# Four small loads ahead of q's, in a linear-attention and feed-forward kernel on one Trainium2 core

## The chip, the cores and the metric

The kernel runs on one core of one Trainium2 chip. The metric is the device time of one execution in microseconds; lower is better. Engines are called as the profile calls them: PE is TensorE (matmuls; PEld is its weight load), DVE is VectorE, ACT is ScalarE, POOL is GpSimd, SP is SyncE, which here issues loads and stores.

## The reference

Inputs are q, k, v of shape (8, 8, 576, 64), w_in of (512, 2048) and w_out of (2048, 512), all float32. What is computed:

```
q_s = softmax(q) over the 64 columns          k_s = softmax(k) over the 576 rows
kv  = einsum('bhsd,bhse->bhde', k_s, v)
a   = einsum('bhsd,bhde->bhse', q_s, kv)
x   = a.transpose(0, 2, 1, 3).reshape(4608, 512)
h   = x @ w_in ;  g = h * sigmoid(h) ;  out = g @ w_out
```

## The kernel before

A batch of q, k or v is loaded in two halves of four heads each (`load`, lines 146 to 150): 128 partitions with two rows of 9 x 64 floats, 576 KB. For each half the exponentials are taken on ACT (`exp_q` L161, `exp_k` L166), q's row sums and their reciprocals on DVE (L205, L209), and q is scaled by them (L214); v is cast to bfloat16 with a column of constants beside it (`vcast`, L142 and L144). q is transposed on PE (L232) and copied out of PSUM (`trcopy`), the products k x v follow on PE (L246), then they are divided by k's sums (`kvcopy`, L257 and L259), multiplied by q (L280) and copied as x into XT (`xt_evac`).

The feed-forward part then works on x in nine chunks of 512 tokens, with the first batch's 576 columns as an exception (`wide_mm`, L305, 16 blocks of 128 columns of w_in). From the second chunk on, both matrix products are done in seven block products in place of eight (L423, L501), so DVE makes sums and differences of weights and inputs. Weights are held as float16: their loads cast from float32 and are issued by POOL (`load_w1` L562, `load_w2` L568).

The order of all work is written by hand: the head is plain code (lines 543 to 619), and behind it the string ORDER names one operation after the other. In the head, SP issues six loads of the first batch one behind the other: q's two halves, k's first, v's first, k's second, v's second. All six go through one hardware queue. ACT starts with the load of its table and an exponential of one element, `dummy`. POOL makes the identity matrix for the transposes and then copies one element of k's first half into `gate` (L577), which holds its queue until that half has landed; only then it issues the five loads of w_in, then q's loads of the second batch, w_out and so on. PE runs matmuls on a tile of zeros (`heat`, L559) in its idle stretches: 20 at the start, then 7, 3 and 2 between the steps of the first batch.

The tile h1 is one of three scratch tiles of 128 x 1024 floats in the pool `mp`. In the kernel before it is first written at L186, at 30.29 us.

Of the kernel before, what the change touches and what calls it, by code (L numbers as in the profile page):

```python
# [8 lines left out]
FP32 = mybir.dt.float32  # L9
# [61 lines left out]
def kernel(  # L71
# [9 lines left out]
    nc = tc.nc  # L81
# [9 lines left out]
    TCH = 512  # L91
# [15 lines left out]
    mp = ctx.enter_context(tc.tile_pool(name="mp", bufs=2))  # L107
# [38 lines left out]
    def load(b, name, src, cc, eng):  # L146
        t = ld.tile([128, 2, J * D], FP32, name=name)
        st[b][name, cc] = t
        x = src[b].rearrange("(g r) (p j) d -> g (r p) (j d)", r=2, j=J)
        eng.dma_start(out=t, in_=x.rearrange("g x y -> x g y")[:, 2 * cc:2 * cc + 2, :])  # L150
# [391 lines left out]

    nc.vector.memset(dummy, 0.0)
    nc.vector.memset(warm, 0.0)
    nc.scalar.activation(out=dummy, in_=dummy, func=ACT.Exp)
    make_identity(nc, ident_f)
    for name, src in (("qt", q), ("kt", k)):
        load(0, name, src, 0, nc.sync)
        if name == "qt":
            load(0, name, src, 1, nc.sync)  # L550
# [154 lines left out]
    for t in range(1, NCH):  # L705
# [6 lines left out]
        for g in range(2):  # L712
            n = f"{t}.{g}."
# [123 lines left out]
```

## Time and profile before

| | us |
|---|---|
| median of 3 runs (258.03 to 258.7) | 258.57 |
| the profiled execution | 258.52 |
| its span, first to last instruction | 256.5 |
| PE busy | 248.3 (97%) |
| DVE busy | 205.5 (80%) |
| ACT busy | 190.9 (74%) |
| POOL busy | 66.3 (26%) |
| moved by DMA | 45.89 MB, mean 179 GB/s |

PE's share is that of matmuls in flight, the ones on zeros among them. The granted TensorE clock is full in all 40 slices of the span. In the page's chain of work that ended last, PE has 50% of the span and "issue", time in which an engine waited for nothing that the profile shows, 32%. The DMA engines are busy, with short dips, from about 2 to 48 us. A share of DMA time above 1 means that packets overlap on an engine.

### The profile page before, as it was taken

The page shows a single profiled execution, that of the slowest core. Times are in us where ns is not written, and L with a number is a line of the kernel's source. Part 1 is how long each engine was busy: PE and PEld are TensorE (multiplying, and loading weights), DVE is VectorE, ACT ScalarE, POOL GpSimd, SP SyncE. Part 2 cuts the span into 40 slices and gives each one's busy share as a digit, 9 for nine tenths or more (in the row PEclk, how much of TensorE's full clock was granted, in tenths as well). Part 3 has the DMA queues.
Part 4 walks back from the last instruction along what each step waited for, and adds up shares of the span by engine and source line. Part 5 has one row for each costly group of instructions (what it writes and reads, how often), then busy time and mean ns, then how long its engine had stood idle before and what let it go on. Part 6 is the DMA issues. An engine that isn't in the chain of part 4 may idle for free.

```text
span 256.5 us, 6456 instructions
## 1 busy us (share of the span) xinstructions
PE 248.3 (97%) x2732; PEld 204.3 (80%) x2732; DVE 205.5 (80%) x276; ACT 190.9 (74%) x225; POOL 66.3 (26%) x64
## 2 busy tenths in 40 slices
PE   8799999999999999999999999999999999999992
PEld 3367746757888888888888888888888888888881
DVE  2858999987999989998998986996569837886750
ACT  4766876998999999999879979736597557565211
POOL 1653592630541440430082040006000000000023
PEclk9999999999999999999999999999999999999999
DMA  7999999979969928995956850030807000700454
GB/s 249 344 180 296 302 301 301 347 162 393 365 162 266 400 87 216 361 306 127 310 223 110 218 202 0 3 82 3 174 3 164 3 0 4 164 3 0 87 130 113
DMA packets 35900, 45.89 MB, mean 179 GB/s; under 512 B 16240, under 2 KB 20912, under 8 KB 35872
## 3 DMA queue, kind: packets, MB, share of 16 engines
q1 hardware_dynamic: 29328, 33.50, 44.8%
q0 software_dynamic: 6224, 11.73, 17.9%
q8 instruction: 21, 0.34, 0.5%
q10 hardware_dynamic: 320, 0.26, 0.5%
q14 instruction: 7, 0.06, 0.1%
HBM read 36.70 MB, written 9.44 MB: 180 GB/s over the span
## 4 chain that ended last, share of the span: by engine, by line
PE 50%; issue 32%; DVE 6%; DMA 5%; POOL 5%; ACT 0%; POOLq 0%; DVEq 0%; ACTq 0%
PE PS L423 21%; PE PS L501 19%; DMA qt<-in_q_dram 5%; PE PS L443 4%; PE PS L333 2%; POOL eq L214 2%; PE PS L246 2%; POOL W L562 1%; POOL out_dram L789 1%; PE PS L280 1%; DVE S L475 1%; DVE XS L381 1%; DVE GT L321 1%; DVE XT L144 1%; DVE zq L205 0%
## 5 line engine op out<-in xcount | busy, mean ns | idle before, releaser
L401 DVE TENSOR_TENSOR h<-PS,h 128x1024 f32<-128x1024 f32 (+1 forms) x45 | 54.1, 1204 | 8.9 <-PE PS L423 7.9
L501 PEld LDWEIGHTS <-GT 128*128 128x128 f16 x512 | 50.1, 98 | 5.9
L423 PEld LDWEIGHTS <-WS 128*128 128x128 f16 x480 | 46.7, 98 | 6.5 <-issue 0.6
L407 ACT ACTIVATE GT<-h 128x1024 f16<-128x1024 f32 (+1 forms) x45 | 46.8, 1049 | 1.0 <-DVE h L401 0.7
L501 PE MATMUL PS<-W,GT 128*128 128x256 f16 x384 | 47.3, 273 | 0.0
L423 PE MATMUL PS<-XS,WS 128*128 128x256 f16 (+1 forms) x360 | 45.0, 272 | 0.0
L142 ACT COPY h<-PS 128x1024 f32<-128x1024 f32 (+1 forms) x31 | 31.1, 1004 | 17.1 <-PE PS L423 16.0
L501 PEld LDWEIGHTS <-S 128*128 128x128 f16 x384 | 37.1, 98 | 4.6
L423 PEld LDWEIGHTS <-W 128*128 128x128 f16 x360 | 35.2, 98 | 4.4
L214 POOL TENSOR_TENSOR eq<-eq,rzq 128x1152 bf16<-128x1152 bf16 x13 | 27.4, 2117 | 37.8 <-DVE rzq L209 37.0
L501 PE MATMUL PS<-T,S 128*128 128x256 f16 x256 | 32.2, 273 | 0.0
L144 POOL CAST vaug<-vt 128x1152 bf16<-128x1152 f32 x12 | 15.5, 1306 | 60.4 <-DMA vt<-in_v_dram 59.6
L423 PE MATMUL PS<-XT,W 128*128 128x256 f16 (+1 forms) x240 | 29.7, 272 | 0.0
L144 DVE COPY h<-PS 128x1024 f32<-128x1024 f32 (+1 forms) x14 | 17.0, 1213 | 8.8 <-PE PS L423 3.9
L205 DVE TENSOR_REDUCE zq<-eq 128x18 f32<-128x1152 bf16 x14 | 18.8, 1341 | 4.1 <-ACT eq L161 3.9
L789 POOL DMA_DIRECT2D out_dram<-ow x7 | 3.8, 542 | 70.6 <-DVE ow L771 70.0
L161 ACT ACTIVATE eq<-qt 128x1152 bf16<-128x1152 f32 (+1 forms) x18 | 18.8, 1054 | 2.7 <-DMA qt<-in_q_dram 2.5
L166 ACT ACTIVATE ek<-kt 128x1152 bf16<-128x1152 f32 x16 | 18.6, 1162 | 1.8 <-DMA kt<-in_k_dram 1.7
L407 ACT ACTIVATE GT<-PS 128x1024 f16<-128x1024 f32 (+1 forms) x15 | 15.2, 1013 | 6.1 <-PE PS L423 6.1
L501 PE MATMUL PS<-T,GT 128*128 128x256 f16 x128 | 16.3, 273 | 0.0
L501 PE MATMUL PS<-W,S 128*128 128x256 f16 x128 | 16.1, 273 | 0.0
L305 PE MATMUL PS<-XT,W 128*128 128x288 f16 x128 | 15.9, 286 | 0.0
(85 smaller groups left out, 331.0 us busy)
## 6 DMA issues: line engine op xcount, KB each, us to landing
out_dram<-ow SPq DMA_DIRECT2D x64, 128.0 KB, 2.7
qt<-in_q_dram SPq DMA_DIRECT2D x12, 576.0 KB, 6.0
kt<-in_k_dram SPq DMA_DIRECT2D x12, 576.0 KB, 7.2
vt<-in_v_dram SPq DMA_DIRECT2D x12, 576.0 KB, 6.9
qt<-in_q_dram POOLq DMA_DIRECT2D x4, 576.0 KB, 10.1
kt<-in_k_dram POOLq DMA_DIRECT2D x4, 576.0 KB, 13.1
vt<-in_v_dram POOLq DMA_DIRECT2D x4, 576.0 KB, 11.8
W<-in_moe_w_in_dram POOLq DMA_DIRECT2D x3, 512.0 KB, 10.5
```

The costliest lines, as they stand in the source:

```text
L142: eng.copy(out=o, in_=i)
L144: eng.tensor_copy(o, i)
L161: nc.scalar.activation(out=half(st[b]["eq"], cc)[:, :, g0:g1], in_=jgd(b, "qt", cc)[:, :, g0:g1], func=ACT.Exp)
L166: nc.scalar.activation(out=half(ek, cc), in_=jgd(b, "kt", cc), func=ACT.Exp)
L205: nc.vector.reduce_sum(out=z, in_=e, axis=AX.X)
L214: eng.tensor_tensor(out=e, in0=e, in1=r[:, :, :, None].to_broadcast([128, J, 2, D]), op=ALU.mult)
L305: nc.tensor.matmul(out=PS[:, WIDE[fb] + n, 0:S // 2], lhsT=W1[:, c, fb * 128:(fb + 1) * 128], rhs=XTS[0][:, c, n * (S // 2):(n + 1) * (S / ...
L401: nc.vector.tensor_tensor(out=four(t, i), in0=group_bank(t, g), in1=four(t, i), op=ALU.add)
L407: nc.scalar.activation(out=group_out(t, f, n), in_=x, func=ACT.Silu, scale=1.0 / XS)
L423: nc.tensor.matmul(out=PS[:, bank + p // 2, (p % 2) * HT:(p % 2) * HT + width(t)], lhsT=a[:, c, p * 128:(p + 1) * 128], rhs=bb[:, c, 0:wid ...
L443: nc.tensor.matmul(out=PS[:, 2 + tb, :], lhsT=GTS[t % 2][:, fc, tb * 128:(tb + 1) * 128], rhs=W2[:, fc, :], start=(fc == 0), stop=(fc == N ...
L501: nc.tensor.matmul(out=PS[:, bank, m * HN:(m + 1) * HN], lhsT=a[:, fc, m * 128:(m + 1) * 128], rhs=bb[:, fc, :], start=(first and fc == 0) ...
```

## The change

Four loads are added at the head of the kernel. Each reads 16 floats (64 bytes) from 16 places: of k's first batch (the first row of each half head, 16 places 72 KB apart), of w_in (every 32nd row, 256 KB apart), of w_out (every 128th row, 256 KB apart) and of v's first batch (as k). They go into 16 partitions of the tile h1, 64 columns in all, and nothing reads them. ACT issues those of k and w_in, ahead of its table load; POOL issues those of w_out and v, behind the identity matrix and ahead of `gate`. Nothing else is changed; every engine's other instructions keep their order.

```diff
     nc.vector.memset(dummy, 0.0)
     nc.vector.memset(warm, 0.0)
+
+    seen = mp.tile([128, 2 * TCH], FP32, name="h1", bufs=1)[0:16, 0:64].rearrange("p (a n) -> p a n", a=4)
+    nc.scalar.dma_start(out=seen[:, 0], in_=k[0].rearrange("h (a s) d -> (h a) s d", a=2)[:, 0, 0:16])
+    nc.scalar.dma_start(out=seen[:, 1], in_=w_in.rearrange("(a r) f -> a r f", a=16)[:, 0, 0:16])
     nc.scalar.activation(out=dummy, in_=dummy, func=ACT.Exp)
     make_identity(nc, ident_f)
+    nc.gpsimd.dma_start(out=seen[:, 2], in_=w_out.rearrange("(a r) o -> a r o", a=16)[:, 0, 0:16])
+    nc.gpsimd.dma_start(out=seen[:, 3], in_=v[0].rearrange("h (a s) d -> (h a) s d", a=2)[:, 0, 0:16])
     for name, src in (("qt", q), ("kt", k)):
         load(0, name, src, 0, nc.sync)
```

## The prediction

> **What bounds the kernel now.** I read the page first, then the instructions in order of time for the first 36 us, then half-microsecond windows of the DMA traffic, and last the trace's packet records (start and length of each) where a window dips. From the page: the time of the span, and TensorE's row in 40 slices.
>
> ```profile
> span 256.5 us, 6456 instructions
> PE   8799999999999999999999999999999999999992
> ```
>
> TensorE is full from the third slice to the last. So the kernel is a head and then a packed stream of matmuls, and this change can touch only the head. Next the head, instructions in order of time (start, duration, engine, line, operation; in brackets the idle time before it and what ended that):
>
> ```profile
> 0.73 1.28 ACT L545 ACT_TABLE_LOAD   x1 [0.73 <-PEq L821]
> 0.74 0.97 SPq L150 DMA_DIRECT2D qt<-in_q_dram  x2
> 4.32 1.16 ACT L161 ACTIVATE eq<-qt 128x1152 bf16<-128x1152 f32 x1 [2.09 <-DMA qt<-in_q_dram]
> 5.52 1.35 DVE L205 TENSOR_REDUCE zq<-eq 128x18 f32<-128x1152 bf16 x1 [3.78 <-ACT eq L161]
> 8.49 1.16 ACT L166 ACTIVATE ek<-kt 128x1152 bf16<-128x1152 f32 x1 [1.42 <-DMA kt<-in_k_dram]
> 8.52 0.18 POOL L577 COPY gate<-kt 1x1 f32<-1x1 f32 x1 [7.21 <-DMA kt<-in_k_dram]
> ...
> 11.97 0.29 DVE L259 TENSOR_TENSOR kvn<-PS,rz 128x128 bf16<-128x128 f32 x1
> 12.68 0.82 PE L559 MATMUL PS<-XS 128*128 128x512 f16 x3
> 12.94 0.76 DVE L144 CAST vaug<-vt 128x576 bf16<-128x576 f32 x1 [0.68 <-DMA vt<-in_v_dram]
> 13.66 0.56 PE L246 MATMUL PS<-vaug,ek 64*64 64x65 bf16 x36 [0.16 <-ACT vaug L142]
> ```
>
> And the same view further on, where the packed stream begins:
>
> ```profile
> 15.20 15.89 PE L305 MATMUL PS<-XT,W 128*128 128x288 f16 x128
> 19.15 11.63 PEld L305 LDWEIGHTS <-W 128*128 128x128 f16 x96 [0.17 <-DMA W<-in_moe_w_in_dram]
> ```
>
> The reader should see two chains into 13.66. One starts where q's first load lands (4.32): exp, then VectorE without a break from 5.52 to 12.26 (11.97 + 0.29), then a product and three filler matmuls on TensorE. The other comes from v's second load, for which VectorE idles 0.68. The stream at L305 then starts matmuls 0.122 us apart; its only gap, at 19.15, costs 0.04 by the starts.
>
> Last, the DMA traffic in windows (busy time of PE, PEld, DVE, ACT, POOL, clock, DMA share, GB/s):
>
> ```profile
> 5.00:5.50 0.50, 0.50 (x4) 0.24 (x3) 0.00 (x0) 0.48 (x1) 0.00 (x0) 1.00 1.12 360
> 5.50:6.00 0.50, 0.50 (x4) 0.25 (x3) 0.48 (x1) 0.09 (x1) 0.00 (x0) 1.00 0.83 318
> 6.00:6.50 0.50, 0.50 (x4) 0.20 (x2) 0.50 (x1) 0.50 (x1) 0.00 (x0) 1.00 1.01 387
> 13.50:14.00 0.50, 0.34 (x33) 0.37 (x35) 0.50 (x2) 0.50 (x2) 0.50 (x2) 1.00 1.24 139
> 14.00:14.50 0.50, 0.50 (x30) 0.23 (x16) 0.21 (x3) 0.50 (x2) 0.50 (x1) 1.00 0.74 98
> 14.50:15.00 0.50, 0.44 (x10) 0.14 (x8) 0.50 (x2) 0.30 (x1) 0.37 (x2) 1.00 0.83 115
> 16.00:16.50 0.50, 0.50 (x6) 0.40 (x5) 0.09 (x1) 0.00 (x0) 0.00 (x0) 1.00 1.19 199
> ```
>
> Two dips. The first is where k is first read: two 2304-byte packets took 712 and 744 ns there, where 93 is usual. Of the 16 end-of-load packets of k's first load, 13 are out by 7.04 us and the last at 7.94; v's first load, k's second and v's second keep that lag (15 of v's last 16 by 11.80, the last at 12.47). The second is in the loads of w_in: packets of 407 to 944 ns against 98; of the load that brings the lower half of w_in's first columns, 12 end by 14.38 and the last at 15.90. That load is first used at 16.43; its landing, some 0.45 behind its last packet (12.47 to 12.94 for v), leaves 0.08.
>
> **The change part by part.** All working is against the profiled execution: 258.52 us, 256.5 of it span and 2.0 around it; the median of the three runs is 258.57, so a difference carries over as it is.
>
> ACT issues two loads ahead of its table load. An ACT issue took 0.47 to 0.61 us (L789 on ACT, four at the end). The table load moves from 0.73 to 1.7-2.0, its end from 2.0 to 3.0-3.25, the dummy exp's end to 3.5 at most. The exp of q starts at 4.32, so at least 0.8 us of cover is left: cost 0. Without the cover it would cost one for one.
>
> POOL issues two loads behind the identity mask, which ends at 1.30. Its issues took 0.53 to 0.87 us, so it is done by 3.05. Its next work is the copy at 8.52 that waits for k: 5.4 us of cover, cost 0. Nothing is queued behind them that anyone needs sooner; VectorE's copy of the mask comes from an instruction ahead of them.
>
> SP's queue and every other instruction keep their order. The loads' completion counters are dealt out in turn, so later loads now wait on the new ones (the second POOL load of q's next batch, w_out's first load, the first transposing DMA at 51.6), and the buffer h1 that takes the rows is first written again at 30.29. All those come more than 7 us after the new loads have landed: cost 0.
>
> The DMA engines carry 64 more data packets of 64 bytes and 64 counter packets: 4 and 4 on each engine. A 4-byte packet took 9 ns and a 256-byte one 18, so 0.11 us on each at most, half of it (ACT's two) where q's first load starts. That is the lower bound of what q's load loses, 0.05. Upper bound: the new loads' first reads are as slow as the slow first reads of q itself (eight packets of 428 to 665 ns, from 1.98 us on) and hold q's packets up twice, 1.3. I take 0.15, near the low end, because k's slow reads struck two engines of sixteen. VectorE has no idle time between 5.52 and 12.26, so this is paid one for one.
>
> What it may take away, first place: k's late engine. Without it k lands near 7.5 (7.04 plus the same 0.45) and v's second load near 11.9 (11.40, where 13 of its 16 end, plus 0.45). VectorE then needs no wait at 12.26: 0.68 gone there. What is late next is TensorE itself. The three fillers start 0.22 apart from 12.68, so the product at 13.66 can't start before 13.34: the room is 0.32 by starts (0.16 by the modelled ends). The fillers follow the product that needs VectorE's 11.97, which hangs on q alone. So the gain is 0.32, whatever k and v do. Below it the gain could be 0; above 0.32 this order excludes it while q's landing stands.
>
> Second place: w_in. If the stream starts 0.32 sooner, the load with 0.08 of room and the one at 19.15 with none must come sooner too. k's landing releases all weight loads (the copy at 8.52), so they are issued some 0.9 sooner, and without the slow packets the four late engines give back up to 1.5 us (15.90 against 14.38). I count 0.32 as passed on, and the 0.04 at 19.15 as gone.
>
> The sooner weight loads meet k's and v's last packets. On the last engine v's 16 packets took 1.49 us (10.98 to 12.47) beside weight packets, and q's second load 1.49 alone (16 x 93 ns), so I count nothing. The Trainium skill, DMA: Bandwidth & Descriptors, section on queues, rings and completion order, says that an engine takes turns between the queues it has work for, a packet of some 9 to 17 descriptors at a time; at half rate from 10.1 on v would land near 12.7, the gain would be 0.2 and the sum below 258.45 instead; the 1.49 us here does not show the halving.
>
> v and w_out: v's first packets took at most 211 ns and w_out's at most 187, where 98 is usual, so touching them brings 0.
>
> Sum: -0.32 - 0.04 + 0.15 = -0.21; 258.57 - 0.21 = 258.36, say 258.35.
>
> **The rivals.**
>
> *Slower: q's first load loses its place.* Place: 0.73 to 2.4 us, where ACT issues beside SP's first issue (0.74) and the cold reads of k and w_in arrive at the engines with q's. Price: X on q's landing and on everything behind it, 0.32 of it covered at best; X is 1.3 by two slow reads in a row, or 0.94 to 1.22 by two ACT issues (0.47 to 0.61) that go first. At 1.3: +0.98, 259.55. It decides from X = 1.1. For it: q's own reads lost up to 0.57 (665 less 93) at that very spot. Against: SP and ACT issues overlapped near 249.5 us with 0.47 and 0.61, little more than alone. The Trainium skill, Perfetto Trace Analysis, section on the HWDGE DMA instruction, speaks against the change here: the block that makes the descriptors is shared by the two engines and locked for one at a time, which would make q's issue wait; these overlapping issues show a wait of 0.14 at most.
>
> *It does nothing.* The slow packets come from something else than first reads, as v's missing ones and those from 55.8 us on suggest; or each engine needs its own first read. Then only q's 0.05 to 0.3 stays: 258.7.
>
> *Faster beyond the room.* The slow first packets of q are a matter of the first traffic of any kind, and the new loads take them: q's load ends at 3.93, and 1.84 + 16 x 93 ns would be 3.33. Then 0.60 + 0.32 + 0.04 = 0.96, 257.6. Against: the new loads are issued at the same moment as q's, not sooner.
>
> **How the numbers follow.** Forecast 0.43 (its own range 258.1 to 258.7), nothing 0.12, slower 0.31, faster 0.14. A change within 0.3%, 0.78 us, is about what a measurement of this kernel can't tell from none. Forecast and nothing lie inside it: same 0.55; slower 0.31; faster 0.14. The range goes to 257.7, which leaves half of the faster case out, and to 259.6, just beyond the slower one at X = 1.3, which leaves about a third of that case out.
>
> **What would show it.** Right: the exp of q within 0.2 of 4.32; the copy that waits for k near 7.6; VectorE's wait of 0.68 for v gone or below 0.2; the product at 13.66 moved to 13.4-13.5; the stream at L305's work starting near 15.0 with no new gap; the dips at 5.5 and 14 filled. Wrong: the exp of q past 5.0 (slower), all of these unmoved (nothing), or the exp of q near 3.8 (faster). The forecast fails also if the stream starts sooner but then stops for w_in at its eleventh matmul.

## The result, and the profile after

The changed kernel is slower: a median of 259.52 us against 258.51 for the kernel before, 22 runs of each. The ratio is 1.0036, with a 95% interval from 1.002 to 1.0051; it is not that of the two medians, which would be 1.0039. So the change costs 0.9 to 1.0 us. The profiled execution of the changed kernel took 260.89 us, the longest of its runs and 1.37 above their median, so its delays are larger than a usual run's. Two experiments below, e10 and e14, have the same head; their profiles show it at a more usual size.

The page of the kernel after has the same shape as before:

```profile
span 259.0 us, 6465 instructions
PE   8799999999999999999999999999999999999992
```

The head, instructions in order of time (start, duration, engine, line, operation; in brackets the idle time before it and what ended that):

```profile
0.74 0.98 SPq L150 DMA_DIRECT2D qt<-in_q_dram  x2
0.74 0.44 ACTq L547 DMA_DIRECT2D h<-in_k_dram  x1
1.22 0.43 ACTq L548 DMA_DIRECT2D h<-in_moe_w_in_dram  x1
1.47 0.65 POOL L551 DMA_DIRECT2D h<-in_moe_w_out_dram  x1 [0.17 <-issue]
1.69 1.28 ACT L549 ACT_TABLE_LOAD   x1 [1.69 <-PEq L827]
2.12 0.51 POOL L552 DMA_DIRECT2D h<-in_v_dram  x1
2.98 0.20 ACT L549 ACTIVATE dummy<-dummy 1x1 f32<-1x1 f32 x1
4.71 1.16 ACT L161 ACTIVATE eq<-qt 128x1152 bf16<-128x1152 f32 x1 [1.53 <-DMA qt<-in_q_dram]
...
9.63 1.16 ACT L166 ACTIVATE ek<-kt 128x1152 bf16<-128x1152 f32 x1 [2.26 <-DMA kt<-in_k_dram]
9.67 0.18 POOL L583 COPY gate<-kt 1x1 f32<-1x1 f32 x1 [7.04 <-DMA kt<-in_k_dram]
...
12.90 0.17 DVE L257 RECIPROCAL rz<-PS 128x2 f32<-128x2 f32 x1 [0.65 <-PE PS L246]
13.10 0.29 DVE L259 TENSOR_TENSOR kvn<-PS,rz 128x128 bf16<-128x128 f32 x1
14.10 0.76 DVE L144 CAST vaug<-vt 128x576 bf16<-128x576 f32 x1 [0.71 <-DMA vt<-in_v_dram]
14.82 0.57 PE L246 MATMUL PS<-vaug,ek 64*64 64x65 bf16 x36 [0.18 <-ACT vaug L142]
```

The issues on ACT and POOL went as costed: ACT still waits 1.53 for q behind its one-element exponential, and POOL waits 7.04 for k behind its issues. The loads did not. q's exponential starts at 4.71 (before 4.32), k's at 9.63 (before 8.49). VectorE, which had no break from 5.52 to 12.26, now idles 0.65 for a product that needs k, and then 0.71 for v (before 0.68). The last product of the head stands at 14.82, which is 1.16 later. In e10 and e14, with the same four loads, k's exponential starts at 8.31 and 8.47 and the stream at 15.43 and 15.22, so most of this 1.16 is this execution's own.

Further on, TensorE's own lines in the same view:

```profile
16.36 15.85 PE L305 MATMUL PS<-XT,W 128*128 128x288 f16 x128
...
48.55 1.02 PE L443 MATMUL PS<-W,GT 128*128 128x512 f16 x4 [0.38 <-DMA W<-in_moe_w_out_dram]
...
55.07 4.70 PE L333 MATMUL PS<-XT,W 128*128 128x448 f16 x24 [0.61 <-ACT GT L407]
```

and the last of them in the kernel before:

```profile
52.79 4.70 PE L333 MATMUL PS<-XT,W 128*128 128x448 f16 x24
```

The stream starts 1.16 later (15.20 before). At 55.07 it is 2.28 later (52.79 before). So about half of what was lost, 1.12 us, was lost inside the stretch that the page paints as full. Two gaps carry most of it: 0.38 for a load of w_out, and 0.61 for ACT, which had itself been kept waiting. Up to the first L501 matmul (62.10 before, 64.55 after) another 0.17 goes. From there to the start of TensorE's last matmul nothing more is lost: 189.31 us before, 189.35 after.

What kept ACT waiting in this execution is the load of the third batch of k (`lk2.0` in ORDER). ACT's exponentials of k, before:

```profile
47.41 1.16 ACT L166 ACTIVATE ek<-kt 128x1152 bf16<-128x1152 f32 x1
48.88 1.16 ACT L166 ACTIVATE ek<-kt 128x1152 bf16<-128x1152 f32 x1 [0.31 <-DMA kt<-in_k_dram]
```

and after:

```profile
50.12 1.16 ACT L166 ACTIVATE ek<-kt 128x1152 bf16<-128x1152 f32 x1 [1.77 <-DMA kt<-in_k_dram]
```

The first needs no wait before, the second waits 0.31: that chain had next to no room already. After, the first waits 1.77.

### The profile page after: what moved, and what is told of

Read it like the earlier page. It is cut to its first block, busy times and chain, and to the rows that moved or that the text cites. A ratio compares the mean times of both kernels' runs of the same rounds, so it can differ in the third digit from the quotient of the medians.

```text
span 259.0 us, 6465 instructions
## 1 busy us (share of the span) xinstructions
PE 250.1 (97%) x2732; PEld 204.8 (79%) x2732; DVE 207.3 (80%) x276; ACT 191.0 (74%) x225; POOL 68.8 (27%) x66
## 4 chain that ended last, share of the span: by engine, by line
PE 46%; issue 30%; DMA 9%; DVE 8%; POOL 3%; ACT 2%; SPq 1%; POOLq 0%; DVEq 0%; ACTq 0%
PE PS L423 19%; PE PS L501 18%; DMA kt<-in_k_dram 5%; DMA vt<-in_v_dram 4%; PE PS L305 3%; PE PS L333 2%; DVE GT L321 2%; PE PS L246 1%; PE PS L280 1%; POOL out_dram L795 1%; POOL eq L214 1%; DVE S L475 1%; SPq L150 1%; DVE WS L371 1%; DVE XS L381 1%
## 5 line engine op out<-in xcount | busy, mean ns | idle before, releaser
L501 PEld LDWEIGHTS <-GT 128*128 128x128 f16 x512 | 50.1, 98 | 5.9
L501 PE MATMUL PS<-W,GT 128*128 128x256 f16 x384 | 47.3, 273 | 0.0
L501 PEld LDWEIGHTS <-S 128*128 128x128 f16 x384 | 37.1, 98 | 4.6
L144 POOL CAST vaug<-vt 128x1152 bf16<-128x1152 f32 x12 | 17.0, 1427 | 59.6 <-DMA vt<-in_v_dram 42.0
L501 PE MATMUL PS<-T,S 128*128 128x256 f16 x256 | 32.2, 273 | 0.0
L501 PE MATMUL PS<-T,GT 128*128 128x256 f16 x128 | 16.3, 272 | 0.0
L501 PE MATMUL PS<-W,S 128*128 128x256 f16 x128 | 16.1, 273 | 0.0
L305 PE MATMUL PS<-XT,W 128*128 128x288 f16 x128 | 15.9, 286 | 0.0
```

The source lines that it names most:

```text
L144: eng.tensor_copy(o, i)
L305: nc.tensor.matmul(out=PS[:, WIDE[fb] + n, 0:S // 2], lhsT=W1[:, c, fb * 128:(fb + 1) * 128], rhs=XTS[0][:, c, n * (S // 2):(n + 1) * (S / ...
L501: nc.tensor.matmul(out=PS[:, bank, m * HN:(m + 1) * HN], lhsT=a[:, fc, m * 128:(m + 1) * 128], rhs=bb[:, fc, :], start=(first and fc == 0) ...
```

## The experiments

Each kernel is the one before with the edit shown, unless it says "after"; the line that makes `seen` is left out of the diffs. In them, K, W, O and V stand for the sources of the four loads of the change: `k[0].rearrange("h (a s) d -> (h a) s d", a=2)`, `w_in.rearrange("(a r) f -> a r f", a=16)`, `w_out.rearrange("(a r) o -> a r o", a=16)`, and K's form for v. One table holds what was measured: the start of q's first exponential, of k's first, of the stream at L305, of the exponential of the third batch of k, and of the first L501 matmul, all from the profiled execution and beside its own time; then the median of the runs against that of the kernel before on the same chip, and the ratio with its 95% interval. There are 12 runs of each, but 22 of the kernel after, 6 of e9 and e14 and 5 of e12.

| kernel | q | k | stream | k, 3rd batch | L501 | profiled | median / before | ratio |
|---|---|---|---|---|---|---|---|---|
| before | 4.32 | 8.49 | 15.20 | 47.41 | 62.10 | 258.52 | | |
| after | 4.71 | 9.63 | 16.36 | 50.12 | 64.55 | 260.89 | 259.52 / 258.51 | 1.0036 [1.002, 1.0051] |
| e1 ACT's two | 4.83 | 8.63 | 15.40 | 48.70 | 62.98 | 259.21 | 259.32 / 258.55 | 1.0018 [0.9998, 1.0037] |
| e2 POOL's two | 4.39 | 9.19 | 15.89 | 48.23 | 62.60 | 258.98 | 258.93 / 258.55 | 1.0023 [1.0, 1.0046] |
| e3 other places | 4.79 | 8.19 | 15.37 | 48.17 | 62.38 | 258.79 | 259.40 / 258.55 | 1.0039 [1.0022, 1.0055] |
| e4 behind SP's six | 4.61 | 8.41 | 15.20 | 48.27 | 62.53 | 258.75 | 258.73 / 258.55 | 0.9998 [0.9978, 1.0018] |
| e5 ACT's two, one place | 4.37 | 8.43 | 15.15 | 47.62 | 62.01 | 258.16 | 258.25 / 258.41 | 0.9996 [0.9978, 1.0013] |
| e6 k alone | 5.06 | 8.18 | 15.64 | 48.14 | 62.40 | 258.50 | 259.35 / 258.41 | 1.0033 [1.0012, 1.0054] |
| e7 w_in alone | 4.68 | 8.82 | 15.53 | 49.52 | 63.77 | 260.87 | 259.36 / 258.41 | 1.0036 [1.0015, 1.0057] |
| e8 ACT's two from q | 4.53 | 8.48 | 15.19 | 48.88 | 63.13 | 259.29 | 259.37 / 258.41 | 1.0025 [1.0004, 1.0046] |
| e9 one more big load | 4.46 | 8.44 | 15.18 | 48.69 | 62.94 | 259.37 | 260.25 / 258.38 | 1.0077 [1.0049, 1.0105] |
| e10 after, one load less | 4.85 | 8.31 | 15.43 | 47.67 | 62.15 | 258.37 | 258.81 / 258.38 | 1.0030 [1.001, 1.0049] |
| e11 before, one load less | 4.37 | 8.22 | 14.95 | 48.83 | 63.08 | 259.57 | 258.43 / 258.38 | 1.0010 [0.9995, 1.0024] |
| e12 k between q's two | 4.43 | 9.98 | 16.70 | 49.64 | 63.90 | 260.26 | 260.17 / 258.38 | 1.0073 [1.0061, 1.0085] |
| e13 before, k sooner | 4.37 | 8.49 | 15.20 | 47.09 | 62.43 | 258.80 | 258.75 / 258.40 | 1.0012 [0.9998, 1.0025] |
| e14 after, k sooner | 4.64 | 8.47 | 15.22 | 47.75 | 63.18 | 259.56 | 259.78 / 258.40 | 1.0050 [1.0031, 1.007] |
| e15 POOL's two, one place | 4.37 | 8.63 | 15.36 | 47.82 | 62.23 | 258.50 | 258.42 / 258.40 | 1.0004 [0.9989, 1.0019] |

**Which issuer: ACT's two alone (e1), POOL's two alone (e2).**

```diff
+    nc.scalar.dma_start(out=seen[:, 0], in_=K[:, 0, 0:16])      # e1: these two
+    nc.scalar.dma_start(out=seen[:, 1], in_=W[:, 0, 0:16])
...
+    nc.gpsimd.dma_start(out=seen[:, 2], in_=O[:, 0, 0:16])      # e2: these two
+    nc.gpsimd.dma_start(out=seen[:, 3], in_=V[:, 0, 0:16])
```

> Only ACT's two loads (k and w_in). Theory 1 (the small loads cost because they take a turn on the DMA engines ahead of q, and bring nothing back): q's first load lands near 4.7 instead of 4.32, the whole train of six loads is 0.3 to 0.4 later, time +0.3 to +0.4 over before. Theory 2 (the rows read first do make the later loads quicker, and POOL's two loads spoil it): k's landing (the copy that waits for it) comes nearer than 8.5, time 0 to -0.3. Theory 3 (the issue on ACT holds up SP's first issue): SP's first issue longer than 0.46.

> Only POOL's two loads (w_out and v). Theory 1: q lands at 4.3 as before, k's landing is late by 0.6 to 0.8 (near 9.2), because these packets come between q's second load and k's first; time +0.5 to +0.7. Theory 2: v and w_out had no slow first reads, so nothing is gained and 64-byte packets cost little: time 0 to +0.1.

ACT's two delay q (4.83) and move the median by 0.77 of the change's 1.01. POOL's two, which come later, leave q alone (4.39) and move the median by 0.38; by the ratios it is 0.47 and 0.59. Neither interval excludes no change, so the prices can't be read from these two alone. In the profiled execution of e2 it is k that comes late (9.19). But e3, e10 and e14, with the same two issues of POOL, have k at 8.19, 8.31 and 8.47, so it is not shown that POOL's loads delay k. The Trainium skill, DMA: Bandwidth & Descriptors, section on issuing engines not being separate DMA queues, says that loads from any engine run on the same 16 DMA engines and interleave there. The trace of e2 agrees: POOL's 64-byte packets go out from 5.01 to 8.00 us, among those of SP's loads and behind q's first.

**Does it matter what they read? (e3)** The same four loads, from batches of k and v that are needed only at the end.

```diff
+    nc.scalar.dma_start(out=seen[:, 0], in_=K7[:, 0, 0:16])     # K7, K6: K's form for k[7], k[6]
+    nc.scalar.dma_start(out=seen[:, 1], in_=K6[:, 0, 0:16])
...
+    nc.gpsimd.dma_start(out=seen[:, 2], in_=V6[:, 0, 0:16])     # V6, V7: for v[6], v[7]
+    nc.gpsimd.dma_start(out=seen[:, 3], in_=V7[:, 0, 0:16])
```

> The same four loads from the same queues, but of places that the first batch doesn't use: k's last two batches and v's. Theory 1 (where they read doesn't matter): the same as the changed kernel, +0.8 to +1.2 over before. Theory 2 (reading the right places gives something back): worse than the changed kernel by 0.3 or more, +1.3 to +1.6.

No: 259.40, with an interval that excludes no change, and q at 4.79. So the cost doesn't hang on k, v or the weights being read ahead. k's exponential, at 8.19, comes sooner than in the kernel before, though nothing had touched its places.

**Is it the place in the order? (e4)** The four loads issued by SP, behind its six.

```diff
         load(0, name, src, 0, nc.sync)
...
+    nc.sync.dma_start(out=seen[:, 0], in_=K[:, 0, 0:16])   # and W, O, V
```

> The four loads of the change, issued by SP behind its six loads of the first batch, so ahead of nothing but the weights. Theory 1: no cost and no gain, within 0.2 of before; q lands at 4.3, k near 8.5. Theory 2: the weights' slow packets near 14 us go, the stream at L305 has no gap, time -0.1 to -0.3.

Behind the six loads they cost nothing that can be measured (0.9998). The slow packets at 5.2 to 5.4 us and at 14.3 to 14.7 us stay as they were.

**The issue, or the sixteen places? (e5, e15)** ACT's two with one place each, and POOL's two with one place each. The issuing instructions stay; the work of the DMA engines shrinks from all sixteen to one.

```diff
+    nc.scalar.dma_start(out=seen[0:1, 0], in_=K[0:1, 0, 0:16])    # e5
+    nc.scalar.dma_start(out=seen[0:1, 1], in_=W[0:1, 0, 0:16])
...
+    nc.gpsimd.dma_start(out=seen[0:1, 2], in_=O[0:1, 0, 0:16])    # e15
+    nc.gpsimd.dma_start(out=seen[0:1, 3], in_=V[0:1, 0, 0:16])
```

> ACT's two loads alone, but each of one place, so that one DMA engine carries them and fifteen don't. Theory 1a (the packets themselves hold the engines that carry them): DMA share from 2.0 to 2.5 us back near 0.8 (0.25 with 16 places), q lands at 4.3 to 4.5, time 0 to +0.2 over before. Theory 1b (the issue on a second queue holds q's load back, whatever it carries): share there stays at 0.25 to 0.35, q lands at 4.7 to 4.8, time +0.5 as with 16 places.

> POOL's two loads alone, each of one place, on one engine. If POOL's part of the loss (k's landing at 9.2, time +0.5) is made by the sixteen engines' packets, as ACT's is: k lands at 8.3 to 8.6, time 0 to +0.2. If it is made by POOL's issue itself: k lands near 9.2, time +0.4 to +0.6.

Both cost nothing that can be measured: 0.9996 and 1.0004, q at 4.37 in each. So ACT's issues are free and its sixteen places are not; for POOL's two the contrast with e2 (1.0023 [1.0, 1.0046]) is too small to say so. One place means one packet and one DMA engine at once: which of the two makes it free was not parted. The half microsecond after q's load begins shows it. In windows (busy time of PE, PEld, DVE, ACT, POOL, clock, DMA share, GB/s), the kernel before:

```profile
2.00:2.50 0.50, 0.50 (x3) 0.17 (x2) 0.00 (x0) 0.22 (x2) 0.00 (x0) 1.00 0.80 180
```

the kernel after:

```profile
2.00:2.50 0.50, 0.50 (x3) 0.17 (x2) 0.00 (x0) 0.50 (x1) 0.50 (x2) 1.00 0.34 83
```

e1, ACT's two with sixteen places:

```profile
2.00:2.50 0.50, 0.50 (x3) 0.18 (x2) 0.00 (x0) 0.50 (x1) 0.00 (x0) 1.00 0.25 42
```

e5, the same two with one place:

```profile
2.00:2.50 0.50, 0.50 (x3) 0.17 (x2) 0.00 (x0) 0.50 (x1) 0.00 (x0) 1.00 0.64 152
```

Of the share of 0.80, 0.34 and 0.25 are left with sixteen places, 0.64 with one. The packet records agree: q's 2304-byte packets begun by 3.0 us are 132 before, 126 in e5, 96 after and 85 in e1. The 64-byte packets themselves are recorded with 8 or 11 ns each. But in the kernel after nine of k's sixteen go out at 1.80 to 1.88 and the other seven only at 2.51 to 2.87.

**One load, or two? (e6, e7)** The load of k alone, and that of w_in alone, both on ACT.

```diff
+    nc.scalar.dma_start(out=seen[:, 0], in_=K[:, 0, 0:16])    # e6
...
+    nc.scalar.dma_start(out=seen[:, 1], in_=W[:, 0, 0:16])    # e7
```

> ACT's load of k alone. Theory 1: it is the one that goes ahead of q (its packets went out at 1.80, those of w_in behind q's at 3.6), so q lands at 4.7 to 4.8 as with both; time +0.3 to +0.5. If the two add up, q lands near 4.5 and the time is +0.2.

> ACT's load of w_in alone. It is now the first on its queue. Theory 1 (any small load ahead of q costs the same): q lands at 4.7 to 4.8, time +0.3 to +0.5. Theory 2 (reading w_in's places first helps the weight loads): the slow packets near 14 us go and the stream at L305 runs without a gap, time 0 to +0.2 in spite of the late q.

One load costs as much as four, as far as the intervals tell: 259.35 and 259.36, both intervals above 1, and about twice the 0.3 to 0.5 that was expected. The price is paid once, for the first load of sixteen places that goes ahead of q. The places of w_in lie 256 KB apart, those of k 72 KB, and it makes no difference.

**Is it that k is read too early? (e8)** ACT's two loads read the sixteen places of q's own first load.

```diff
+    nc.scalar.dma_start(out=seen[:, 0], in_=Q[:, 0, 0:16])    # Q: K's form for q[0]
+    nc.scalar.dma_start(out=seen[:, 1], in_=Q[:, 0, 0:16])
```

> ACT's two loads alone, reading 16 places of q's first batch, which q's own first load reads at the same moment. Theory 1a' (the time goes into first reads of places that nothing else reads): q lands at 4.3 to 4.4, time 0 to +0.1. Theory 1 (a turn on the engines costs the same wherever it reads): q lands at 4.7 to 4.8, time +0.4 to +0.6.

This run parts two things. First, q's slow first packets are gone: by 3.0 us none took more than 268 ns, where the kernel before had 651, 649 and 665. That would fit a place being read faster once it has been read ahead, but it is a single execution: the longest such packet is 415 ns in the kernel after, which reads nothing of q ahead, and 562 to 753 in the other fifteen profiles. Second, it doesn't help: seven of the first load's 64-byte packets go out only at 2.60 to 2.71, q lands no sooner (4.53), and the median is 259.37. Its stream starts as in the kernel before, and the time is lost later. TensorE's lines of e8:

```profile
15.19 4.09 PE L305 MATMUL PS<-XT,W 128*128 128x288 f16 x32
19.51 2.56 PEld L305 LDWEIGHTS <-W 128*128 128x128 f16 x22 [0.54 <-DMA W<-in_moe_w_in_dram]
...
53.83 4.70 PE L333 MATMUL PS<-XT,W 128*128 128x448 f16 x24 [0.46 <-ACT GT L407]
...
63.13 1.04 PE L501 MATMUL PS<-W,GT 128*128 128x256 f16 x8
```

and ACT's of e8:

```profile
48.88 1.17 ACT L166 ACTIVATE ek<-kt 128x1152 bf16<-128x1152 f32 x1 [1.08 <-DMA kt<-in_k_dram]
```

against this one of TensorE before:

```profile
62.10 1.04 PE L501 MATMUL PS<-W,GT 128*128 128x256 f16 x8
```

The stream starts 0.01 sooner and the first L501 stands 1.03 later: 0.39 of it is lost by the first L443 matmul, where w_in is waited for at 19.51, and 0.62 on the way into L333. So it is refuted that whatever is lost is lost ahead of the stream. From here on the theory was that the loads are one train on DMA engines that have hardly any idle time until 48 us, and that a train which starts late arrives late: at w_in (19.51), at w_out, and at k's third batch, for which ACT waits.

**Is the train on the path? (e9)** The kernel before, with one load of 512 KB that nobody needs, issued by POOL in the middle of the train (its head is untouched).

```diff
-    lv1.0 h8 v6 w11 v8 h9 lv1.1 w10 ...
+    lv1.0 h8 v6 w11 v8 h9 lv1.1 xl w10 ...
+    def extra():
+        t = mp.tile([128, 2 * TCH], FP32, name="h2", bufs=1)
+        nc.gpsimd.dma_start(out=t, in_=k[7].rearrange("h (a s) d -> (h a) (s d)", a=16)[:, 0:2 * TCH])
+    op("xl", extra)
```

> The kernel before with one more load of 512 KB on POOL's queue behind v's of the second batch, near 27 us, into scratch that nothing reads; 8 packets of 4 KB on each engine, about 1.3 us of the engines' time. Theory A (a delay of the loads is carried by full engines to k's third batch at 47.4 us, and TensorE follows that landing): start of the stream at L305 as before, 15.2; exp of k's third batch at 48.5 to 48.7; time +0.7 to +1.0. Theory B (only the head up to 15.2 us counts): time within 0.2 of before.

It is: 260.25, which is 1.87 more, for 0.52 MB. That is about twice the 0.7 to 1.0 that was expected, from six runs between 259.11 and 261.52; the profiled execution, 259.37, is 0.85 more. ACT's line of e9, and TensorE's:

```profile
48.69 1.16 ACT L166 ACTIVATE ek<-kt 128x1152 bf16<-128x1152 f32 x1 [0.92 <-DMA kt<-in_k_dram]
```

```profile
62.94 1.04 PE L501 MATMUL PS<-W,GT 128*128 128x256 f16 x8
```

The head of e9 is that of the kernel before (stream at 15.18), and the delay shows at w_out's load (0.37) and at k's third batch (0.45 on the way into L333). The packet records show the train: the extra load is issued at 27.38, its 128 packets go out at 35.28 to 38.53, and at a median of 165 ns they are 1.3 us of each engine. POOL issues k's third batch at 37.53, as before (37.48), and its exponential starts 1.28 later. Engines at work are not the only way in which a delay is passed on, though. In the kernel after, e1, e7 and e12 POOL's issue of that load is late too, by 0.87 to 1.53, for POOL's queue stands still for landings on its way: in the kernel before, its issue at 19.40 comes after 1.90 of waiting for w_in.

**Does a shorter train hide the cost? (e10, e11)** The second half of the second batch of v isn't loaded, in the kernel after (e10) and before (e11). Heads 4 to 7 of that batch are computed with the first batch's v, so the work is the same and only the load of 576 KB is left out.

```diff
-    lv1.0 h8 v6 w11 v8 h9 lv1.1 w10 ...
+    lv1.0 h8 v6 w11 v8 h9 w10 ...
+    st[1]["vt", 1] = st[0]["vt", 1]
```

> The changed kernel without the load of v's second half of the second batch (that batch's heads 4 to 7 use v of the first batch instead), so 1.4 us less for the engines to do before k's third batch. Theory A: the late loads no longer reach TensorE through k's third batch; of the +1.0 of the change only the late head is left, time +0.2 to +0.6 over before. Theory B: +1.0 as with the change.

> The kernel before without the same load of v, the partner of the run ahead. Theory A and B: 0 to -0.3 against before, since k's third batch is only just in time there. What counts is the distance between the two: 0.3 to 0.6 by theory A, 1.0 by theory B.

The two medians stand 0.38 apart, where after and before stand 1.01 apart. That is the direction of the theory, which asked for 0.3 to 0.6, but the intervals, 1.0030 [1.001, 1.0049] and 1.0010 [0.9995, 1.0024], overlap. The pair is inconclusive. e11 also carries a warning: in its profiled execution, with no small loads at all, the train was late by itself (k's third batch at 48.83, 259.57 in all, where its median is 258.43). Single executions differ in this place by as much as the change costs.

**Only k, and out of q's way (e12).** The one small load that was meant to help, issued by SP between q's two.

```diff
         load(0, name, src, 0, nc.sync)
         if name == "qt":
+            nc.sync.dma_start(out=seen[:, 0], in_=K[:, 0, 0:16])
```

> Only the small load of k, issued by SP on q's own queue between q's first and second load. If its cost is its place ahead of q and it does take slow first reads off k, then q lands at 4.3 to 4.4, k near 8.0 to 8.3 and the time is 0 to -0.3. If a small load stops its engine wherever it stands, q's second load and k are late by 0.5 and the time is +0.3 to +0.5.

This is much worse than where the change put it: 260.17, where 0 to -0.3 was hoped for and +0.3 to +0.5 named as the other way. q's first load keeps its place (4.43), and its second lands 2.56 later than the kernel before has it. From the order of time of e12:

```profile
8.47 1.16 ACT L161 ACTIVATE eq<-qt 128x1152 bf16<-128x1152 f32 x1 [2.88 <-DMA qt<-in_q_dram]
...
9.98 1.16 ACT L166 ACTIVATE ek<-kt 128x1152 bf16<-128x1152 f32 x1 [0.35 <-DMA kt<-in_k_dram]
```

and e12's windows there, to hold against the 396, 396, 360, 318 and 387 GB/s of the same five half microseconds in the kernel before:

```profile
4.00:4.50 0.50, 0.50 (x2) 0.15 (x1) 0.00 (x0) 0.07 (x1) 0.00 (x0) 1.00 0.73 217
4.50:5.00 0.50, 0.50 (x2) 0.15 (x1) 0.00 (x0) 0.50 (x1) 0.00 (x0) 1.00 0.74 198
5.00:5.50 0.50, 0.50 (x3) 0.18 (x2) 0.00 (x0) 0.50 (x1) 0.00 (x0) 1.00 0.87 217
5.50:6.00 0.50, 0.50 (x3) 0.23 (x2) 0.38 (x1) 0.09 (x1) 0.00 (x0) 1.00 0.72 194
6.00:6.50 0.50, 0.50 (x4) 0.24 (x3) 0.50 (x1) 0.00 (x0) 0.00 (x0) 1.00 0.84 249
```

The engines are busy here (0.72 to 0.87) but move half to two thirds as much: ten 2304-byte packets begun from 3.99 to 5.74 took 566 to 1907 ns, where 93 is usual. Why one small load does this to the load behind it stays open.

**Can the train be taken off the path? (e13, e14)** `lk2.0` moved ahead of `lq2.0` and the work between, in the kernel before (e13) and after (e14).

```diff
-    WS1.4 W2c2 tr1.0 v14 lq2.0 p4 tc1.0a tc1.0b lq2.1 n1.1 p5 W2d p6 lk2.0 T1 ...
+    WS1.4 W2c2 tr1.0 v14 lk2.0 lq2.0 p4 tc1.0a tc1.0b lq2.1 n1.1 p5 W2d p6 T1 ...
```

> The kernel before with the first load of k's third batch issued ahead of q's third batch in place of behind it and w_out's last. In every profile so far where the exp of that load starts after 48.1, TensorE's stream at L501 starts 14.25 us behind it. Theory A (TensorE's stream follows that landing): this exp no longer waits for its load; time 0 to -0.3 against before. Theory B (only the start of the stream at L305 counts): 0 as well; what tells them apart is the distance to the next run.

> The changed kernel with the same one load moved up. Theory A: more than half of the change's +1.0 goes, time +0.2 to +0.5 against before, what is left being the later start of the stream at L305 (0.3 to 0.7). Theory B: the whole +1.0 stays, +0.9 to +1.1 against the kernel before with the load moved up.

It can't be, in this way. The two stand 1.03 apart, as after and before do. That is a miss for the theory of the train, which expected more than half of the 1.0 to go. It is the number of the other theory, by which only the start of the stream counts; but the stream's start is not the reason, for it is the same in both (15.20 and 15.22). TensorE's lines of e13:

```profile
47.37 1.02 PE L443 MATMUL PS<-W,GT 128*128 128x512 f16 x4 [0.36 <-DMA W<-in_moe_w_out_dram]
```

and of e14:

```profile
16.80 5.26 PEld L305 LDWEIGHTS <-W 128*128 128x128 f16 x44 [0.48 <-DMA W<-in_moe_w_in_dram]
...
48.12 1.02 PE L443 MATMUL PS<-W,GT 128*128 128x512 f16 x4 [0.45 <-DMA W<-in_moe_w_out_dram]
```

k's third batch comes sooner, and w_out's last load, now behind it, comes late instead, in both. The 0.75 by which e14's first L501 matmul (63.18) stands behind e13's (62.43) is nearly all lost ahead of either load: e14's stream stops for w_in behind its first ten matmuls, and against e13 it is 0.47 late at 31 us, 0.65 at 39 and 0.75 at 48.

No kernel of this study is measurably faster than the one before.

## Why the prediction was wrong

It forecast 258.35, which is 0.21 sooner and too little to tell from no change, and gave "slower" 0.31. The time, 259.52, is inside its range and on the side it held less likely. In the terms of its sum: the gains of 0.32 and 0.04 did not come, the 0.15 at q was some 0.4, and what was lost behind the head had no term.

**"This change can touch only the head."** This is the step that failed first. It rests on the 40 slices, which stand at 9 in both kernels while 1.12 us disappear inside them: a slice is 6.5 us long, and gaps of 0.4 and 0.6 leave its digit at 9. Behind the head TensorE still waits for loads, and in the kernel before they come with little room: w_in's near 17 to 20 us, w_out's near 47, and k's third batch, whose exponential on ACT waits 0.31 in its second half and leads to the matmuls at L333. Which of them takes the time differs from profile to profile. Against the kernel before:

- From the start of the stream to the first L443 matmul (30.93 before), where w_in is waited for: e1 loses 0.63, e7 0.69, e8 0.39, e14 0.41, and e11, without any small load, 0.42.
- From there to the product near 47 us: e9 and e13 lose 0.37, the kernel after 0.39 and e14 0.65, most of it for w_out, and e11 0.24.
- On the way into L333, behind k's third batch: the kernel after, e3, e4, e7, e8, e9, e11 and e12 lose 0.27 to 0.77, the others nothing.

So e1 loses most of its 0.88 at w_in, and goes into L333 with no gap:

```profile
17.11 2.56 PEld L305 LDWEIGHTS <-W 128*128 128x128 f16 x22 [0.62 <-DMA W<-in_moe_w_in_dram]
...
53.67 4.70 PE L333 MATMUL PS<-XT,W 128*128 128x448 f16 x24
```

In the fourteen profiles beside e13 and e14 that have k's third batch in its place and a wait of the first exponential for it, the first L501 matmul comes 14.21 to 14.48 behind that exponential, whenever the stream began (14.95 to 16.70). In eight of them it is the load that holds TensorE; in the other six (e1, e2, e5, e6, e10, e15) the load is just in time, and the interval alone does not show what set it. From the first L501 matmul to the end, 16 of 17 profiled times lie 196.10 to 196.49 behind it (e7: 197.10), so all that is lost is lost ahead of it. e8 and e14 lose their time without losing any ahead of the stream, and e9 makes a delay of this size with an untouched head.

**"I take 0.15"** for q's first load, with bounds of 0.05 and 1.3. The eight profiles in which a load of sixteen places goes ahead of q have it at 4.53 to 5.06, a median of 4.75; the others, before among them, at 4.32 to 4.61, a median of 4.37. So it is late by some 0.4: within the bounds, but more than twice what was taken. And it is not paid one for one: in e1, e3, e6, e8, e10 and e14 the stream starts later than before by what q is late beyond 0.32, to within 0.03 (e6: 0.74 and 0.44), and not at all where q is late by less. That 0.32 is the room the prediction had worked out between its two chains. By these chains 0.4 at q leaves about 0.1 at the stream, so the head alone does not explain the 1.01. The reason for the low value, that slow reads struck only two engines of sixteen, took the wrong row. What goes with the cost is not slow packets but that seven of the sixteen small packets in the kernel after went out 0.6 to 1.1 us behind the first, while the share of DMA time fell to 0.34.

**"The gain is 0.32"** at k, and 0.04 at w_in. It did not come. After q landed late there was nothing to gain from an earlier k, and in the profiled execution k came 1.14 later (in e10 and e14, with the same head, 0.18 and 0.02 sooner). The cause that was to bring it failed: k's slow packets stayed, 384 to 729 ns near 5.4 to 5.9 us and one of 1105 at 7.0; so did w_in's, 607 to 828 ns at 11.3 to 12.8. Only e8, one execution, suggests that a first read can be made faster by a read ahead, for q's.

**What held.** ACT's issues, the table load and POOL's issues cost nothing, by their covers in the profile after and by e5 and e15. Touching v and w_out brought nothing. The slower rival had the right place (0.73 to 2.4 us, q's load) and the wrong price and way. It asked for 1.1 us at q before it would decide, because it too looked only at the head; some 0.4 us at q went with the whole loss. That its time at X = 1.3, 259.55, is almost the measured one is luck. Its second cause, ACT's issues going first, is excluded by e5. The Trainium skill, Perfetto Trace Analysis, section on the HWDGE DMA instruction, has the descriptor block locked for one engine at a time. In this trace SP's first issue took 0.457 us with ACT's issue beside it and without, while a later one, at 2.28, took 0.74 instead of 0.47. The rule does not decide this case.

**The signs it named.** q within 0.2 of 4.32: 4.71. The copy that waits for k near 7.6: 9.67. VectorE's wait for v gone: 0.71. The product at 13.4 to 13.5: 14.82. The stream near 15.0: 16.36. The dip at 5.5 filled: the share there is 0.79 (0.83 before); that at 14 can't be compared, since the head is 1.16 later by then. Each of them says that the gain didn't come, and none but the last looks behind 16.4 us. That last one, a stop for w_in at the stream's eleventh matmul, is absent in the kernel after; e1 and e14 have it (0.62 and 0.48 of wait behind ten matmuls), and so does e11, without any small load (0.55).

**What stays open.** Why part of the small packets goes out so late and q's load mostly stands still meanwhile, whether it takes sixteen engines or only sixteen packets, and why e12's load cuts the rate behind it to half or two thirds. That a delay of the train at 3 us is the one that is seen at 48 is argued from e8, e9 and the table; it was not followed packet by packet. By 48 us the kernel after had moved 13.5 MB, e1 13.5 and e8 13.7, the kernel before 13.9 and e5 14.0. But e3 had moved 14.0 and e6 13.8, and their exponentials of k's third batch still start 0.7 late. And e11's execution shows that a train can come late without any small load. e10 and e11, which were to settle how much of the cost the train carries, did not.

## What to carry to other kernels

A row of nines for TensorE doesn't say that it has no gaps: look also for the lines that wait a few tenths for a load inside the full stretch, and for loads that come with no room, for there a delay of the loads can come out again. Here a small load of sixteen places, ahead of a large one whose landing is waited for, was not small, whatever it read; with one place it was free. And where the profiled execution is far from the median, or one chain varies from run to run as this train does, judge a mechanism by several profiles side by side.

## What was not expected of the hardware

Loads of 16 times 64 bytes, with packets recorded at 8 or 11 ns, took the DMA share of the half microsecond from 2.0 us from 0.80 to 0.25 (e1). In the median they cost some 0.8 to 1.0 us, whether ACT issued one of them (e6, e7) or there were four. The same issues with one place each cost nothing (e5, e15). Behind a small load on the same queue, where q's second load runs, the engines moved 194 to 249 GB/s for 2.5 us in place of 318 to 396 (e12). And q's first packets, up to 665 ns in the kernel before, took at most 268 in the one execution in which their places had been read ahead (e8), and at most 415 in the kernel after, which reads none of them; for k and w_in no such effect was seen.
